# Reordering the first units of a chunked RWKV-7 kernel with a mixture of experts behind it

## The chip, the core and the metric

The kernel runs on one core of a Trainium2 chip. The metric is the device time of one execution in microseconds. Three timed executions of the kernel before gave 1142.85, 1146.27 and 1148.96 us; the median, 1146.27 us, is the time before. The execution that left the profile took 1141.15 us, and its span in the profile is 1139.1 us. The engines are called as in the profile: PE is TensorE (matrix products), DVE is VectorE, ACT is ScalarE, POOL is GpSimd, SP is SyncE, which issues most of the transfers.

## What is computed

The first half of the reference is a recurrence. For each of 4 batches and 8 heads, a 40x40 state goes through 768 tokens:

```python
for t in range(S):
    y[:, :, t] = einsum('bhd,bhde->bhe', r_t, state)
    Sa    = einsum('bhde,bhe->bhd', state, a_t)
    state = state * w_t[:, :, None, :] - einsum('bhd,bhe->bhde', Sa, b_t)
    state = state + einsum('bhd,bhe->bhde', v_t, k_t)
```

The second half takes y, as a matrix x of 3072 tokens by 320 (8 heads of 40), through 4 experts:

```python
p = domain_probs / (domain_probs.sum(-1, keepdims=True) + 1e-09)
for e in range(E):                          # E = 4
    h = np.maximum(x @ w1[e], 0.0)          # 320 -> 1024
    out += p[:, e:e+1] * (h @ w2[e])        # 1024 -> 320
```

All of it is in float32.

## The kernel before, in words

**Units.** The 768 tokens are cut into 12 chunks of 64. A unit is one chunk of two batches (64 + 64 tokens on the 128 partitions, all 8 heads), so there are 24 units; units 0 and 1 are the first chunk of batches 0, 1 and 2, 3. Within a chunk the recurrence becomes products of small matrices and the inverse of a unit triangular 64x64 matrix for each head and batch. Each unit goes through four generators, whose `yield`s are the places where other work can be put between:

- `within` makes what doesn't need the state. It has these steps: the running product of the decays, G (two transposes of rawW, a scan at L401, on DVE); its transpose `pg` on PE and the division `gp`; the scaled keys `n_tok`, `k_tok` and `AT`; their transposes `pNT`, `pKT`; the scores `pc` between R and V (masked on DVE into VC, L382); the scores `pfe` and `pe` (L478 to L485; `pfe` is copied by ACT into F, and `pe` is masked on DVE into ET); the product `pev` of ET and V (copied by ACT into EV).
- `substitute` inverts the 32x32 diagonal blocks of F by forward substitution: ACT and DVE gather `blocks`, DVE transposes them into M (L519) and prepares M and Z (L531, L535). The substitution proper (L540 to L557) runs on DVE for units 0 and 1 and on GpSimd for all others.
- `merge` puts the inverted 32x32 blocks together to 64x64: two transposes on DVE, Qc (L568) and QTc (L570), four copies on GpSimd, then the products `pY` and `pQ` on PE, each followed by copies on ACT.
- `step` takes the state along: `prn` (products with the state, carried in), RH on DVE, `psat` and `pst`, then `pxr` (R with the solution and with the state), masked on DVE into SX, then `pdy`, Y and the new state on DVE, and at last x, transposed by the products `pxT` for the first two chunks and by transfers for the others.

**The experts.** `up` computes relu(x w1) with the products `ph` (L726, L734); `down` of units 0 and 1 computes `po` (L775). From the second chunk on, two units are taken together, with Winograd's form of Strassen's scheme for the second product (`p`, L841), for which `add_weights` (L802) makes sums of w2 on DVE in passing. The weights w1 are streamed from HBM for each unit or chunk in pieces of 640 KB (`load_piece`). All such pieces of work wait in the list `todo`; `mix(n)` takes n of them.

**The order.** Each engine runs its own queue in order. The order is written out by hand in two parts, L939 to L1014 for the first units and the loop L1021 to L1087 for the rest, by how many steps of which generator are run when (`run(gen, n)`). A scheduler may move an instruction between that and the queue, unless `keep_in_program_order` pins it. Among the pinned ones are Qc and QTc, the blocks and M, the masks of VC and ET up to unit 3, and the G, `n_tok`, `k_tok` and AT of the first units.

In pass u of the loop, unit u goes through its step (`s`), unit u+1 through its merge (`m`) and the beginning of its step (`s_next`), unit u+2 through the scores (`w`) and the substitution, and unit u+3 begins. What is left of unit u+1's `within` at the pass's start (`w_next`) is its last product, `pev`. `gap(n)` gives PE pieces of the experts' work; gap 0 is the first. The call `run(sum_ops, ...)` in it makes sums of w2 at the places that `sums_at` names.

**Spare products.** `keep_warm(n)` (L933) puts n products of the identity with itself into PE's queue, each in two passes (two records). Their result isn't used. There are three such calls: 16 at the start, 10 behind the first `pg`, and 18 in front of the first merge's `pY`.

**Buffers.** All accumulators but those of the experts come from one ring of five banks (`big`, L72). `banks` takes two. A new taker waits for the readers of the one that is five takes older. For unit 0, `pe` has banks of its own; for all others it shares those of `pfe`. rawW, rawA, rawV and rawR are one buffer each: the next unit's transfer into them waits for the transpose that reads them.

Of the kernel before, what the change touches and what calls it, by code (L numbers as in the profile page):

```python
# [15 lines left out]
def kernel(  # L16
# [154 lines left out]
    def begin(u):  # L171
        q = Unit()
        q.u, q.c, q.bp = u, u // (B // 2), u % (B // 2)
        q.b = [2 * q.bp, 2 * q.bp + 1]
        q.start, q.end = q.c == 0, q.c == NC - 1
        q.n = {}
        units.append(q)
        return q
# [9 lines left out]
    def load_raw(q, names):  # L188


        moves = []
        for x in names:
            q.n["raw" + x] = t = raw[x]()
            heads = srcs[x].rearrange("b h t e -> (b h) t e")[q.b[0] * H:(q.b[1] + 1) * H, q.c * L:(q.c + 1) * L, :]
            heads = heads.rearrange("n (x two) e -> x n (two e)", two=2)
            for r in range(2):
                if x in "RV":

                    sets = ((slice(0, 8, 2), slice(r, 16, 4)), (slice(1, 8, 2), slice(3 - r, 16, 4)))
                else:  # L200
                    sets = ((slice(0, 8), slice(r, 16, 2)),)
                for n, hs in sets:
                    for y, w_ in enumerate((D + Q, 2 * D - Q)):
                        o = slice(64 * r + Q * y, 64 * r + Q * y + Q)
                        moves.append(lambda eng, out=t[o, n, 0:w_], in_=heads[:, hs, Q * y:Q * y + w_]: eng.dma_start(out=out, in_=in_))
        return moves
# [10 lines left out]
    def go(moves, eng=None):  # L217
        for move in moves:
            move(eng or nc.sync)
# [43 lines left out]
    def load_piece():  # L263

        k = len(pieces)
        e, x = k // 2 % E, k % 2
        if k in in_sums:
            t = sums[in_sums[k]]
        else:
            t = sb.tile([P, PIECE], FP32, name="w1p", tag="w1p", bufs=2)  # L270
        q = Piece()
        q.main = t[:, 0:2 * HF * P].rearrange("p (g c) -> p g c", g=2)
        q.last = t[:, 2 * HF * P:PIECE].rearrange("p (f c) -> p f c", c=P)
        cols = slice(x * HF * P, (x + 1) * HF * P)
        moves = [(q.main, moe_w1[e, 0:2 * P, cols].rearrange("(g p) c -> p g c", p=P))]
        for i in range(2):
            half_cols = slice((2 * x + i) * HF // 2 * P, (2 * x + i + 1) * HF // 2 * P)
            moves.append(
                (q.last[i * DT:(i + 1) * DT], moe_w1[e, 2 * P:DM, half_cols].rearrange("d (f c) -> d f c", c=P))
            )  # L280
        for to, src in moves:
            tc.keep_in_program_order(nc.sync.dma_start(out=to, in_=src))
        pieces.append(q)
# [14 lines left out]
    def load_w2(e):  # L298
        tc.keep_in_program_order(nc.sync.dma_start(out=w2_sb[e][:], in_=moe_w2[e].rearrange("(f p) d -> p f d", p=P)))
# [62 lines left out]
    def banks(name):  # L362
        return [big(f"{name}{x}") for x in range(2)]
# [20 lines left out]
    def within(q):  # L384

        n = q.n
# [91 lines left out]
        pf = quadrants(p, 0, BY_TOKENS, L, lambda j, s, i: (  # L478
            s, i ^ s, j, of_slots(q.AT, s, j, i), of_pairs(NT, s, j, i),
        ))  # L480
        if q.u == 0:
            p = banks("pe")
        pe = quadrants(p, NJ * L, BY_TOKENS, L, lambda j, s, i: (
            s, i, j, of_pairs(KT, s, j, i), of_slots(q.AT, s, j, i),
# [78 lines left out]
    def merge(q):  # L563


        Qc = sb.tile([P, H, Q], FP32, name="Qc", tag="q", bufs=2)
        QTc = sb.tile([P, H, Q], FP32, name="QTc", tag="q", bufs=2)
        tc.keep_in_program_order(nc.vector.transpose(out=dealt(Qc[:]), in_=q.Z))  # L568
        tc.keep_in_program_order(
            nc.vector.transpose(  # L570
                out=QTc[:].rearrange("p h r -> p (h r)"), in_=Qc[:].rearrange("p h c -> p (h c)"),
            )
        )
        q.QT = QTs()
        for i in range(P // Q):
            ins = nc.gpsimd.tensor_copy(out=q.QT[quarter(i), :, quarter(i % 2)], in_=QTc[quarter(i)])  # L576
            tc.keep_in_program_order(ins)
        yield

        py = big("pY")  # L580
        for h in range(H):
            for i in (1, 3):
                nc.tensor.matmul(  # L583
                    out=py[quarter(i - 1), h * Q:(h + 1) * Q], lhsT=q.F[quarter(i), h, 0:Q],
                    rhs=QTc[quarter(i), h, :], start=True, stop=True,
                )
        Y = sb.tile([P, H, Q], FP32, name="Yq")
        for i in (0, 2):
            nc.scalar.copy(out=Y[quarter(i)].rearrange("p h t -> p (h t)"), in_=py[quarter(i), 0:H * Q])
        yield  # L590

        pq = big("pQ")
        for h in range(H):
            for i in (0, 2):
                nc.tensor.matmul(  # L595
                    out=pq[quarter(i), h * Q:(h + 1) * Q], lhsT=Qc[quarter(i), h, :],
                    rhs=Y[quarter(i), h, :], start=True, stop=True,
                )
        for i in (0, 2):
            nc.scalar.copy(out=q.QT[quarter(i), :, quarter(1)], in_=by(pq[quarter(i), 0:H * Q], Q))  # L600
        yield
# [306 lines left out]
    def mix(n):  # L908

        for piece in todo[:n]:  # L910
            piece()
            begin_later(3 if n > 1 else 6)
        del todo[:n]

    def run(gen, n=99):
        if gen is None:
            return
        for _ in range(n):
            if next(gen, gen) is gen:
                break  # L920
# [3 lines left out]
    def begin_step(u):  # L924
        q = units[u]
        if q.bp == 0:
            chunks_x[q.c] = sb.tile([P, 3, 2 * P], FP32, name="xT", tag="xT", bufs=2)
        q.xT = chunks_x[q.c][:, :, q.bp * P:(q.bp + 1) * P]
        return step(q, q.xT)
# [3 lines left out]
    def keep_warm(n):  # L933

        for _ in range(n):
            ins = nc.tensor.matmul(out=warm[:, 0:P], lhsT=ident[:], rhs=ident[:], start=True, stop=True)
            tc.keep_in_program_order(ins)

    ws = [within(units[u]) for u in range(3)]  # L939
# [23 lines left out]
    m, s = merge(units[0]), begin_step(0)  # L963
# [6 lines left out]
    load_piece()  # L970
    run(ws[1], 1)
    run(norm, 1)
    keep_warm(18)
    run(ws[1], 1)
    run(m)
    run(ws[2], 1)
    run(norm)
    load(units[2], "BK")
    go(load_raw(units[2], "A"))
    go(load_raw(begin(3), "W"))  # L980
    load_w2(0)
    load_piece()
    load_piece()
    load_w2(1)
    load_piece()
    run(s, 2)
    run(ws[1], 1)
    run(s)
    run(ws[1], 2)

# [8 lines left out]
    m, s = merge(units[1]), begin_step(1)  # L999
# [15 lines left out]

    sparse = range(4 * 1, 4 * 4 + 2)

    sums_at = {4 * 2 + n: 1 for n in range(1, 11)}
    sums_at.update({4 * 4 + 3: 2, 4 * 5 + 0: 3, 4 * 5 + 1: 2, 4 * 5 + 2: 3})
    sum_ops = (None for e in range(E) for _ in add_weights(e))  # L1020
    for u in range(1, NU):  # L1021
        q = units[u]
        m = s_next = w = w_next = iter(())
        if u + 1 < NU:
            m, s_next = merge(units[u + 1]), begin_step(u + 1)
            w_next = ws[u + 1]
        if u + 2 < NU:
            w = ws[u + 2]

        def gap(n, pieces=None):  # L1030
            at = 4 * u + n
            run(sum_ops, sums_at.get(at, 0))
            mix((1 if at in sparse else 2) if pieces is None else pieces)

        run(w_next)
        run(s, 1)
        gap(0)


        early = u < 5  # L1040
        if early:
            run(s, 1)
        run(w, 1)
        run(s)
        if u == 1:
            mixture_of_unit(q)
        elif q.bp:
            mixture_of_chunk(units[u - 1:u + 1], chunks_x[q.c])
        begin_later(len(later))
        run(w, 1)  # L1050
        if not early:
            run(m, 1)
        gap(1)

        if u + 3 < NU:
            go(load_raw(begin(u + 3), "WA"))
            load(units[u + 3], "WBKV")
            later.extend(load_raw(units[u + 3], "VR"))
        run(w, 2)
        if early:  # L1060
            run(m, 1)
        else:
            run(s_next, 1)
            run(m, 1)
        gap(2)

        if not early:
            run(m, 1)
        run(w, 1)
        if not early:  # L1070
            run(s_next, 1)
        if u + 2 < NU:
            substitute(units[u + 2], nc.gpsimd)
        run(w, 1)
        if u + 3 < NU:
            ws.append(within(units[u + 3]))
            run(ws[u + 3], 1)
        if early:
            run(m, 1)
            run(s_next, 1)  # L1080
            run(m)
            gap(3, 1)
            run(s_next, 1)
            mix(0 if 4 * u + 3 in sparse else 1)
        else:
            gap(3)
        s = s_next  # L1087
# [31 lines left out]
```

## Time and profile before

| engine | busy, us | share of 1139.1 us |
|---|---|---|
| PE | 1099.4 | 97% |
| DVE | 757.8 | 67% |
| POOL | 473.6 | 42% |
| ACT | 338.0 | 30% |

| stretch, us | PE busy, us | mean granted clock |
|---|---|---|
| 0 to 20 | 10.81 | 0.98 |
| 20 to 40 | 15.53 | 0.59 |
| 40 to 60 | 17.62 | 1.00 |
| 60 to 160 | 95.02 | 1.00 |
| 160 to 180 | 16.29 | 1.00 |
| 180 to 200 | 15.14 | 0.75 |
| 200 to 260 | 57.67 | 1.00 |
| 260 to 1100 | 836.3 | 1.00 |
| 1100 to 1139 | 35.00 | 1.00 |

The first table says that PE is the engine with the least room. The second says where the room is: in the first 260 us, in which the pipeline of units fills. The granted clock is the share of its full speed at which PE was allowed to run.

A row of the profile's time line reads: start, duration, engine, line of the kernel, operation, out<-in, shapes, count, and in brackets how long the engine stood idle before it and which instruction of which engine ended that. PE counts two records for one float32 product.

### The profile page before, as it was taken

Reading aid. Unit: us, or ns where it says so; the run is one execution under the profiler, and the core shown is the slowest. Engines: PE = TensorE matmul, PEld = TensorE weight load, DVE = VectorE, ACT = ScalarE, POOL = GpSimd, SP = SyncE. Lnnn points to the kernel's source line nnn. Section 1 sums busy time; section 2 is a strip of 40 time slices with the busy share of each in tenths; the row PEclk is TensorE's granted clock in tenths of the full one; section 3 lists DMA queues with packets and bytes.
Section 4 is the critical chain, followed back from the end, with each engine's and each line's share of the span. In section 5 each row is a group of like instructions: output and inputs, shape, how many; then the busy total and the mean of one; then the engine's idle time right before and its main releaser. Section 6 shows DMA issues by size and latency. Waiting matters only on the chain.

```text
span 1139.1 us, 38245 instructions
## 1 busy us (share of the span) xinstructions
PE 1099.4 (97%) x16036; PEld 976.6 (86%) x16036; DVE 757.8 (67%) x1553; ACT 338.0 (30%) x860; POOL 473.6 (42%) x1221
## 2 busy tenths in 40 slices
PE   6899997999999999999999999999999999999998
PEld 5777776888998989889899898888989898888887
DVE  8756647697767768667677677677677586553343
ACT  2333333333233232332332332332332322311110
POOL 4005626662724635625526526437337246340000
PEclk8899998999999999999999999999999999999999
DMA  7784643254263454444453453443543442231330
GB/s 118 213 245 124 131 99 78 65 132 101 76 146 89 107 128 100 119 122 101 115 121 83 123 118 86 118 102 84 139 102 87 117 110 64 75 90 55 105 92 12
DMA packets 268867, 122.16 MB, mean 107 GB/s; under 512 B 213737, under 2 KB 242073, under 8 KB 268697
## 3 DMA queue, kind: packets, MB, share of 16 engines
q1 hardware_dynamic: 265416, 119.12, 42.7%
q8 instruction: 126, 2.06, 0.8%
q10 hardware_dynamic: 3280, 0.61, 0.3%
q14 instruction: 45, 0.36, 0.1%
HBM read 111.79 MB, written 3.93 MB: 102 GB/s over the span
## 4 chain that ended last, share of the span: by engine, by line
PE 87%; DVE 4%; SPq 2%; DMA 2%; POOL 2%; ACT 2%; issue 1%; DVEq 0%; ACTq 0%
PE ph L734 29%; PE p L841 28%; PE ph L726 9%; PE pdy L371 4%; PE pfe L371 2%; PE psat L371 2%; PE pxr L371 2%; PE prn L371 2%; PE po L775 2%; PE pQ L595 1%; PE pc L371 1%; PE pY L583 1%; PE pev L371 1%; POOL Z L557 1%; PE pg L335 1%
## 5 line engine op out<-in xcount | busy, mean ns | idle before, releaser
L734 PE MATMUL ph<-xT,w1p 128*128 128x256 f32 (+1 forms) x1520 | 344.1, 379 | 2.2 <-issue 2.2
L734 PEld LDWEIGHTS ph<-xT,w1p 128*128 128x128 f32 x1520 | 274.3, 190 | 65.1 <-issue 27.3
L544 POOL TENSOR_TENSOR Z<-M,Z 128x62 f32<-128x62 f32 (+7 forms) x352 | 143.3, 407 | 368.6 <-DVE M L535 336.0
L557 POOL TENSOR_TENSOR Z<-Z 128x31 f32<-128x31 f32 (+7 forms) x704 | 257.2, 365 | 55.2
L835 DVE TENSOR_TENSOR a<-hs 128x512 f32<-128x512 f32 x220 | 152.4, 710 | 128.2 <-ACT hs L739 128.2
L739 ACT ACTIVATE hs<-ph 128x512 f32<-128x512 f32 (+1 forms) x208 | 115.7, 564 | 295.5 <-PE ph L734 295.1
L841 PE MATMUL p<-sums,a 128*128 128x160 f32 x1056 | 165.1, 299 | 0.0
L752 DVE SCALAR_TENSOR_TENSOR osb<-p,gate,osb 128x320 f32<-128x320 f32 (+1 forms) x243 | 107.9, 481 | 74.9 <-PE p L841 70.9
L841 PEld LDWEIGHTS p<-sums,a 128*128 128x128 f32 x1056 | 152.9, 190 | 2.3
L726 PE MATMUL ph<-xT,w1p 64*128 64x256 f32 (+1 forms) x760 | 110.1, 398 | 1.2 <-issue 1.1
L841 PE MATMUL p<-w,hs 128*128 128x160 f32 x704 | 102.9, 299 | 0.0
L841 PE MATMUL p<-w,a 128*128 128x160 f32 x704 | 102.8, 299 | 0.0
L841 PEld LDWEIGHTS p<-w,hs 128*128 128x128 f32 x704 | 100.3, 190 | 2.2
L841 PEld LDWEIGHTS p<-w,a 128*128 128x128 f32 x704 | 98.0, 190 | 0.0
L576 POOL COPY QT<-QTc 32x256 f32<-32x256 f32 x96 | 51.6, 537 | 111.5 <-DVE QTc L570 103.7
L726 PEld LDWEIGHTS ph<-xT,w1p 64*128 64x128 f32 x760 | 67.8, 187 | 14.4 <-issue 4.4
L519 DVE STREAM_TRANSPOSE M<-blocks 128x1024 f32<-128x1024 f32 x24 | 47.0, 1957 | 23.1 <-ACT blocks L516 23.0
L414 DVE RECIPROCAL gp<-gp 128x320 f32<-128x320 f32 x24 | 51.7, 2152 | 0.8
L504 ACT COPY EV<-pev 64x160 f32<-64x160 f32 x96 | 23.4, 286 | 66.8 <-PE pev L371 66.3
L371 PE MATMUL pdy<-VC,k_tok 64*64 64x104 f32 (+1 forms) x768 | 41.6, 260 | 0.1
L600 ACT COPY QT<-pQ 32x256 f32<-32x256 f32 x48 | 17.4, 362 | 79.3 <-PE pQ L595 78.8
L626 ACT COPY SN<-prn 128x256 f32<-128x256 f32 x44 | 15.7, 370 | 84.1 <-DVE RH L621 81.9
(148 smaller groups left out, 1364.0 us busy)
## 6 DMA issues: line engine op xcount, KB each, us to landing
w1p<-in_moe_w_dram SPq DMA_DIRECT2D x95, 512.0 KB
w1p<-in_moe_w_dram SPq DMA_DIRECT2D x190, 64.0 KB
w<-in_moe_w_dram SPq DMA_DIRECT2D x4, 1280.0 KB
sums<-in_moe_w_dram SPq DMA_DIRECT2D x9, 512.0 KB
natW<-in_w_dram SPq DMA_DIRECT2D x48, 80.0 KB
natB<-in_b_dram SPq DMA_DIRECT2D x48, 80.0 KB
natK<-in_k_dram SPq DMA_DIRECT2D x48, 80.0 KB
out_dram<-osb SPq DMA_DIRECT2D x46, 80.0 KB
```

The costliest lines, as they stand in the source:

```text
L371: nc.tensor.matmul(out=p[row][half(col), lo + at * out_cols:lo + (at + 1) * out_cols], lhsT=lhsT, rhs=rhs, start=(n == 0), stop=(n == len( ...
L414: pin(nc.vector.reciprocal(out=gp[:], in_=gp[:]))
L519: ins = nc.vector.transpose(out=M[:], in_=cols)
L544: ins = eng.tensor_tensor(out=Z[:, 1:3, 0:n, j + 1:Q], in0=M[:, j:j + 2, None, j + 1:Q].to_broadcast([P, 2, n, m]), in1=Z[:, here, 0:n, j: ...
L557: eng.tensor_tensor(out=z[:, 0], in0=z[:, 0], in1=z[:, x], op=ALU.add)
L576: ins = nc.gpsimd.tensor_copy(out=q.QT[quarter(i), :, quarter(i % 2)], in_=QTc[quarter(i)])
L726: nc.tensor.matmul(out=ph[i][:, f, :], lhsT=w1.last[i * DT:(i + 1) * DT, f, :], rhs=xT[i * DT:(i + 1) * DT, 2, :], start=(f == 0), stop=False,
L734: nc.tensor.matmul(out=ph[i][:, f, :], lhsT=w1.main[:, g, at * P:(at + 1) * P], rhs=xT[:, g, :], start=False, stop=(g == 1 and f == HF // ...
L739: nc.scalar.activation(out=h[:, i * HF // 2:(i + 1) * HF // 2, 0:n], in_=ph[i][:], func=ACTF.Relu,)
L752: nc.vector.scalar_tensor_tensor(out=to, in0=p, scalar=sc, in1=to, op0=ALU.mult, op1=ALU.add)
L835: nc.vector.tensor_tensor(out=t[:], in0=x, in1=y, op=op)
L841: nc.tensor.matmul(out=p[:, n * HD:(n + 1) * HD], lhsT=a[:, f, :], rhs=b[:, f, :], start=(f == 0), stop=(f == HF - 1),)
```

## The change

It has five parts.

1. In front of the first merge stand 2 spare products in place of 18.
2. Unit 2's first step (its G, on DVE) is moved behind unit 0's whole step, so that DVE has unit 0's masks, Y and state first. The transfer of rawW for unit 3, which needs unit 2's G to be done, is moved behind two pieces of w1. The steps of `s` and of unit 1's `within` between them are split anew.
3. `pe` gets banks of its own for units 0 and 1 (`q.start`), not for unit 0 alone.
4. In each first gap of the loop, the third step of `s` (`pxr`, and the products with the state carried in) goes ahead of `w_next` (`pev`, from the scores).
5. In passes 1 and 2 the first step of the merge (Qc and QTc) goes ahead of the scores `pc` of unit u+2, where it came behind them. And the sums of w2 are dealt to slightly earlier gaps.

Parts 1 to 3 are meant to bring unit 0's x, which the experts wait for, forward; part 4 to have unit u's masks under way while PE does `pev`; part 5 to have the merge's transposes done before it is their turn.

```diff
@@ within
-        if q.u == 0:
+        if q.start:
             p = banks("pe")
@@ the first units
     run(norm, 1)
-    keep_warm(18)
+    keep_warm(2)
     run(ws[1], 1)
     run(m)
-    run(ws[2], 1)
+    run(s, 2)
+    run(ws[1], 1)
+    run(s, 1)
     run(norm)
     load(units[2], "BK")
     go(load_raw(units[2], "A"))
-    go(load_raw(begin(3), "W"))
     load_w2(0)
     load_piece()
     load_piece()
+    run(s, 1)
+    run(ws[2], 1)
+    go(load_raw(begin(3), "W"))
     load_w2(1)
     load_piece()
-    run(s, 2)
-    run(ws[1], 1)
     run(s)
     run(ws[1], 2)
@@ the loop
-    sums_at = {4 * 2 + n: 1 for n in range(1, 11)}
-    sums_at.update({4 * 4 + 3: 2, 4 * 5 + 0: 3, 4 * 5 + 1: 2, 4 * 5 + 2: 3})
+    sums_at = {4 * 2 + n: 2 if n == 4 else 1 for n in range(1, 10)}
+    sums_at.update({4 * 4 + 2: 2, 4 * 4 + 3: 3, 4 * 5 + 0: 2, 4 * 5 + 1: 3})
...
+        run(s, 1)
         run(w_next)
-        run(s, 1)
         gap(0)
...
-        run(w, 2)
+        run(w, 1)
+        if u < 3:
+            run(m, 1)
+        run(w, 1)
         if early:
-            run(m, 1)
+            run(m, 1 if u >= 3 else 0)
         else:
             run(s_next, 1)
             run(m, 1)
```

## The prediction

> **What bounds the kernel now.** I read the page first (shares and slices), then TensorE's waits, then the stretches in order of time around the places that the diff moves.
>
> ```profile
> PE 1099.4 (97%) x16036; PEld 976.6 (86%) x16036; DVE 757.8 (67%) x1553; ACT 338.0 (30%) x860; POOL 473.6 (42%) x1221
> PE   6899997999999999999999999999999999999998
> PEclk8899998999999999999999999999999999999999
> ```
>
> TensorE is busy 97% of 1139.1 us, in each slice after the first eight nine tenths or more until the last. From 260 to 1100 us the table by stage gives it 836 busy of 840 us. So a reordering pays or costs only where TensorE idles or runs at a low clock: before about 260 us. What TensorE gains or loses there, the end gains or loses. The slices at 20 to 40 us and about 190 us have a clock under full; one-microsecond stretches place its changes:
>
> ```profile
> 36.00:37.00 1.00, 1.00 (x9) 0.83 0.00 0
> 190.00:191.00 1.00, 0.00 (x0) 0.50 0.82 122
> 200.00:201.00 1.00, 1.00 (x5) 0.91 0.00 0
> ```
>
> (Columns: stretch, its length, TensorE busy and records, granted clock, DMA share, GB/s.) Solving the means for the switch gives half clock from 19.3 to 36.3 us and from 190.0 to 200.2. The spare products stand in the first of these:
>
> ```profile
> 32.43 6.14 PE L936 MATMUL warm<-ident 128*128 128x128 f32 x36
> 32.56 0.45 DVE L570 STREAM_TRANSPOSE QTc<-Qc 128x256 f32<-128x256 f32 x1
> 37.81 0.69 DVE L458 TENSOR_TENSOR AT<-AT,G 128x512 f32<-128x512 f32 x1
> 38.49 0.69 PE L583 MATMUL pY<-QTc,F 32*32 32x32 f32 x32
> ```
>
> QTc, which pY reads, is done at 33.0, but the 18 spare products (36 records) hold the queue until 38.5. They are also the work during which the clock came up.
>
> The third place is unit 2's merge in the loop's pass u = 1, where VectorE waits for GpSimd's substitution:
>
> ```profile
> 110.02 0.70 DVE L223 STREAM_TRANSPOSE RT<-rawR 128x512 f32<-128x512 f32 x1
> 111.62 0.69 PE L371 MATMUL pc<-RT,VT 40*64 40x64 f32 x32
> 112.40 0.77 DVE L382 COPY_PREDICATED VC<-mask_up,pc 128x256 f32<-128x256 int32 x2 [1.68 <-PE pc L371]
> 115.02 0.51 POOL L557 TENSOR_TENSOR Z<-Z 128x8 f32<-128x8 f32 x2
> 115.57 0.62 DVE L568 STREAM_TRANSPOSE Qc<-Z 128x256 f32<-128x256 f32 x1 [2.40 <-POOL Z L557]
> 116.22 0.45 DVE L570 STREAM_TRANSPOSE QTc<-Qc 128x256 f32<-128x256 f32 x1
> ```
>
> Qc sits 2.40 us at the head of VectorE's queue until GpSimd ends at 115.5 (it began at 94.60: 20.9 us). RT, pc and VC, unit 3's scores, had passed before it.
>
> **What the Trainium skill says.** "TensorE: Matmul & The Clock Gate", Part 1 (What's actually happening): the clock is halved by default, is released after about one busy window and taken back after an idle one; windows last 3413 ns and run free. The trace agrees: the switches above lie 17.06, 153.6 and 10.2 us apart, which is 5, 45 and 3 windows. It adds what the page doesn't: 190 to 200 us has TensorE busy from 191.9 on with 32x32 and 64x64 products, and the clock rose only after a window of full-width ones. The same page (Architectural detail, at the engines' queue depths) says that VectorE is strictly first in, first out; the 2.40 us above is that.
>
> **The change part by part**, from the order of instructions that the changed program has.
>
> *16 spare products fewer.* pY can start at about 33.1: 5.4 us earlier. But its successors now run at half clock. Trace pairs, full and half: pY 0.69 and 1.07 us, a group of four transposes 0.60 and 1.06 (pVT at 84.4 and 22.0), pev 0.67 and 1.32. Step by step: pY 33.1-34.2; copy of Y 0.75, pQ about 1.0, copy of QT, so that psat starts at 36.5; psat and pst 2.5 in place of 1.5, to 39.3 (before 42.8); pNT and pKT 2.1 in place of 1.1, to 41.4 (43.8); pxr 1.3, SX's first masked copy done at 43.15 (44.9); pdy, 2.0 us from there in before, 4.0 at half, ends 47.1. Before it ended at 47.03. If the clock comes up midway (a boundary near 43.2), it ends at 45.1; if it stays down to the ph products, pxT, pc, pfe and pe lose another 1 to 2 us. I take no gain at pdy's end; ends: 2.1 earlier to 1.5 later.
>
> *Unit 2's G behind the first x* (38.42 to 41.15, 2.7 us of VectorE). It lay beside pY and pQ. Now it stands between the state, done at 48.7, and VC, which ran at 50.23: VC starts at 51.45. With pe in banks of its own, pe's second bank takes the buffer of pc, which VC must have read: pe waits from 50.4 to 51.9, and behind it stand the ph products. Hidden partly: before, 0.81 us of idle followed at 51.6. F no longer waits for pe, 0.45 us, but M stands behind VC and blocks in VectorE's queue, 52.85 in place of 52.64. pev, now after one bank of products, waits 0.9 us for ET. Against that, TensorE idled 1.72 us at 65.7 for osb, which now stands two instructions earlier. Sum with the first part: about -0.3 us, ends -2.7 and +1.5.
>
> *pxr before pev.* From unit 4 on TensorE is full and both are needed later: 0. In pass 1 it costs: before, 0.72 + 1.16 us of ph stood between po and pev, and still pev waited:
>
> ```profile
> 94.94 0.28 PE L371 MATMUL pev<-VC,ET 64*64 64x40 f32 x2 [0.82 <-DVE ET L382]
> ```
>
> Now 0.69 (pxr) and 0.5 (three ph) stand there: arrival 93.5, wait 1.4, so +0.6. Passes 2 to 4: pxr comes straight after psat and waits some 0.3 us for SaT's copy, pev then covers SX's mask: 0.
>
> *Merge ahead of the scores, u = 1.* VectorE's new order is VT, AT, osb, Qc, QTc, RT, VC. Queued behind Qc's wait are RT and VC; pc waits for RT; everything of TensorE stands behind pc. GpSimd's end doesn't move against TensorE: its start hangs on M, and M on pfe at 87.8, with the same work before. Qc 115.5-116.1, QTc to 116.6, RT to 117.3, pc at 117.35. TensorE gets to pc at 111.62 + 0.6 = 112.2. It stands 5.1 us. pY follows pc by the same work as before, so nothing is given back: QTc was ready for it anyway. Bounds: 4 (GpSimd faster while VectorE stands) to 5.7.
>
> *The same, u = 2.* GpSimd ends at 143.46, VectorE reaches Qc at 142.9: wait 0.5, nothing behind it urgent (VT, for 159.0).
>
> ```profile
> 161.62 0.69 PE L583 MATMUL pY<-QTc,F 32*32 32x32 f32 x32 [0.96 <-DVE QTc L570]
> 163.57 1.91 DVE L519 STREAM_TRANSPOSE M<-blocks 128x1024 f32<-128x1024 f32 x1
> 166.21 0.30 PE L371 MATMUL psat<-QT,RH 64*64 64x64 f32 x2 [1.44 <-DVE RH L621]
> ```
>
> Qc and QTc (0.60 + 0.45) leave VectorE's path to M, RH and psat, and pY no longer waits 0.96: -1.0 us. The wait at 187 (4.86 us, for GpSimd's unit 4) hangs on M too and moves along: 0.
>
> *Clock after the new gap.* The gap at 187 to 191.9 took the clock down; 5.1 us is as long. It holds a whole window of 3.41 in (5.1 - 3.41) / 3.41 = half of the phases, and a nearly empty one in some more; one or two windows at half clock then cost 1.7 to 3.4 us. Estimate from these: +1.0, ends 0 and 3.5.
>
> *The rest.* sums_at moves w2's sums by one place in passes 2 to 5; VectorE has 33% idle: 0. rawW for unit 3 two pieces later: needed by G at 95, 0.
>
> Sum: -0.3 + 0.6 + 5.1 - 1.0 + 1.0 = +5.4 us; with rounding of the pieces 1146.3 + 5.2 = 1151.5.
>
> **The rivals.**
> *Cold all through* (20%): clock low from 19 us until the ph products, and again after the new gap: 1.5 + 0.6 + 5.1 - 1.0 + 3.5 = +9.7, 1156. For it: small products didn't raise the clock at 191.9 to 196.8. Against: pdy fills all four quadrants.
> *No stall* (16%): GpSimd's substitution ends before TensorE needs pc, because TensorE is held up elsewhere or VectorE's idleness lets GpSimd run faster: -0.3 + 0.6 - 1.0 = -0.7, 1145.6. Against: it would need 5 of 20.9 us.
> *Gain carried* (12%), the other side: the clock is up already (the free windows straddle the idle stretch of 14.8 to 20.7), 5 us won at pY, kept to pdy, no stall: -5 - 1.0 = 1140.3. For it: that idle stretch, 5.9 us, misses a whole window in a quarter of phases. It also needs the stall absent.
> Forecast 52%.
>
> **How the numbers follow.** 1151.5 is the forecast's. Half a per cent is 5.7 us, a line at 1152: of the forecast somewhat under half lies above, with the cold rival's 0.2 makes 0.45; faster 0.11; same 0.44. The four times of before spread over 7.8 us (1141.15 to 1148.96). Range: from just under the no-stall case, 1144, to 1157, over the cold case; what is left out is mainly the gain carried.
>
> **What would show it.** Right: in pass 1 TensorE idle about 5 us in front of pc, put down to RT, and Qc waiting some 4.5 us for GpSimd with RT behind it; pY of the first merge at 33 and 1.07 us long; pdy of unit 0 ending near 47; pY of unit 3 without a wait. Wrong: pc of unit 3 without a wait, or pdy of unit 0 ending before 45 at full clock. The forecast falls if the cost of the queue order in pass 1 is under 2 us.

## The result and the profile after

Three timed executions of the changed kernel gave 1161.53, 1162.02 and 1163.34 us, the one that left the profile 1168.7; the median of the four is 1162.68 us. The ratio to the kernel before is 1.0154, with an interval of 1.0116 to 1.0192: some 17.6 us slower. The forecast, 1151.5 us, had the sign and a third of the size, and the time lies above its range. The trace of the kernel after is of the slowest of its four executions, the trace of before is of the fastest: between the two traces lie more than 17.6 us.

The page of the kernel after, the rows that answer to those shown of before (busy time; busy tenths by slice; granted clock by slice):

```profile
PE 1114.9 (96%) x16004; PEld 987.3 (85%) x16004; DVE 755.9 (65%) x1553; ACT 341.9 (29%) x860; POOL 473.2 (41%) x1221
PE   6798998889999999999999999999999999999998
PEclk8798797999999899999999999999999999999999
```

TensorE's busy time rose by 15.5 us although it has 32 records fewer, and in the profiled executions the span rose by 27.8 us (1139.1 to 1166.9), so idle time rose by 12.3. Busy time that grows with less work points to the clock, and the clock's row shows it: counted from 0, slices 0, 1, 3, 4, 6 and 13 stand at 7 or 8, where before 0, 1 and 6 stood at 8. One-microsecond stretches of the kernel after (stretch, length, five engines' busy time, granted clock, DMA share, GB/s) place some of the changes:

```profile
93.00:94.00 1.00, 1.00 (x31) 0.92 (x32) 0.89 (x5) 0.13 (x1) 0.82 (x3) 0.54 0.82 272
113.00:114.00 1.00, 0.19 (x8) 0.19 (x12) 0.76 (x2) 0.00 (x0) 0.69 (x2) 0.78 0.76 122
123.00:124.00 1.00, 1.00 (x42) 0.87 (x34) 0.10 (x1) 0.75 (x3) 0.00 (x0) 0.60 0.91 280
127.00:128.00 1.00, 0.74 (x21) 0.55 (x22) 1.00 (x4) 0.37 (x1) 0.00 (x0) 0.61 0.39 80
```

Solved for the switches as in the prediction, the means give a clock at half from 18.0 to 41.9 us, 93.1 to 96.5, 113.6 to 123.8, 127.2 to 134.0, 175.0 to 185.2, and in four shorter stretches up to 793 us. Before it was at half in two stretches up to 1100 us.

The first merge in the kernel after, where the 16 spare products are gone:

```profile
32.57 1.22 PE L936 MATMUL warm<-ident 128*128 128x128 f32 x4
32.72 0.45 DVE L570 STREAM_TRANSPOSE QTc<-Qc 128x256 f32<-128x256 f32 x1
33.73 1.06 PE L583 MATMUL pY<-QTc,F 32*32 32x32 f32 x32
```

pY starts at 33.73 (before 38.49) and takes 1.06 us at half clock, both as forecast. And pass 1, unit 2's merge, in the kernel after:

```profile
111.48 0.51 POOL L557 TENSOR_TENSOR Z<-Z 128x8 f32<-128x8 f32 x2
112.03 0.61 DVE L568 STREAM_TRANSPOSE Qc<-Z 128x256 f32<-128x256 f32 x1 [2.69 <-POOL Z L557]
113.05 0.71 DVE L223 STREAM_TRANSPOSE RT<-rawR 128x512 f32<-128x512 f32 x1
113.81 1.13 PE L371 MATMUL pc<-RT,VT 40*64 40x64 f32 x32 [2.83 <-DVE RT L223]
```

Qc waits for GpSimd, RT stands behind Qc, and pc waits for RT. This is the forecast's chain, but the wait is 2.83 us and not 5.1, because TensorE itself came late. What the forecast had nothing of is in the table of TensorE's waits (waiting product, what it waited for, us in total, times, longest). Kernel after:

```profile
PE psat L371 <- issue: 7.0, 4, 3.1
PE prn L371 <- issue: 4.1, 2, 2.1
PE ph L726 <- issue: 3.2, 2, 1.9
```

Kernel before:

```profile
PE psat L371 <- issue: 3.1, 3, 1.5
PE ph L734 <- issue: 2.2, 2, 1.1
PE ph L726 <- issue: 1.1, 2, 0.8
```

"issue" means that the profile shows nothing that the engine waited for. All such waits of TensorE make 6.4 us before and 16.0 after.

### The profile page after: what moved, and what is told of

The parts are those of the page before. It is cut to its first block, busy times and chain, and to the rows that moved or that the text cites. A ratio compares the mean times of both kernels' runs of the same rounds, so it can differ in the third digit from the quotient of the medians.

```text
span 1166.9 us, 38162 instructions
## 1 busy us (share of the span) xinstructions
PE 1114.9 (96%) x16004; PEld 987.3 (85%) x16004; DVE 755.9 (65%) x1553; ACT 341.9 (29%) x860; POOL 473.2 (41%) x1221
## 3 DMA queue, kind: packets, MB, share of 16 engines
q8 instruction: 126, 2.06, 0.8%
## 4 chain that ended last, share of the span: by engine, by line
PE 89%; DVE 6%; issue 2%; ACT 1%; DMA 1%; SPq 0%; DVEq 0%; ACTq 0%
PE ph L734 30%; PE p L841 28%; PE ph L726 9%; PE pdy L371 4%; PE po L775 3%; PE psat L371 2%; PE pfe L371 2%; PE pxr L371 2%; PE prn L371 2%; PE pc L371 1%; PE pQ L595 1%; PE pY L583 1%; PE pev L371 1%; PE pNT L335 1%; PE pKT L335 1%
## 5 line engine op out<-in xcount | busy, mean ns | idle before, releaser
L667 ACT COPY RS<-pxr 64x256 f32<-64x256 f32 x88 | 32.2, 366 | 94.9 <-DMA rawR<-in_r_dram 41.8
L414 DVE RECIPROCAL gp<-gp 128x320 f32<-128x320 f32 x24 | 51.6, 2151 | 0.7
L775 PE MATMUL po<-w,hs 128*128 128x320 f32 x128 | 43.2, 486 | 0.0
L371 PE MATMUL pdy<-SX,n_tok 64*64 64x104 f32 (+1 forms) x768 | 40.2, 252 | 2.1 <-DVE SX L382 2.1
```

What stands on the lines that cost most here:

```text
L371: nc.tensor.matmul(out=p[row][half(col), lo + at * out_cols:lo + (at + 1) * out_cols], lhsT=lhsT, rhs=rhs, start=(n == 0), stop=(n == len( ...
L414: pin(nc.vector.reciprocal(out=gp[:], in_=gp[:]))
L775: nc.tensor.matmul(out=po[:], lhsT=hs[e][f // HF][:, f % HF, 0:P], rhs=w2_sb[e][:, f, :], start=(f == 0), stop=(f == NF - 1),)
```

## The experiments

Ratios are to the kernel before, timed on the same chip beside each kernel; each has its 95% interval. A hundredth is 11.4 us.

### Which part costs what

Three kernels leave out parts of the change, and a fourth has one part alone. Without part 5's merge order:

```diff
-        run(w, 1)
-        if u < 3:
-            run(m, 1)
-        run(w, 1)
+        run(w, 2)
         if early:
-            run(m, 1 if u >= 3 else 0)
+            run(m, 1)
```

> The changed kernel with the merge's transposes behind the scores again in passes 1 and 2; TensorE's and ScalarE's queues are the changed kernel's, only VectorE's order differs. Theory (the queue order on VectorE stops TensorE once, and the clock lost in that gap and after it multiplies the loss): the wait of 2.83 us before unit 3's pc goes, and with it the half clock behind it; 1152 to 1156 us. Rival (the products carried in ahead of the scores' do the damage by themselves): under 3 us gained, 1160 or more. Rival (this order is the whole loss): within 3 us of before, 1146.

Measured: 1154.47 us, 1.0078 (1.0051 to 1.0106).

Without part 4:

```diff
-        run(s, 1)
         run(w_next)
+        run(s, 1)
         gap(0)
```

> The changed kernel with pev ahead of pxr again in each first gap. Theory: the half clock at 93 to 96 us and the waits of pdy for RS go, but TensorE still stops for unit 3's RT, now for about 5 us since it gets there earlier; 1153 to 1158 us. Rival (the order in the first gap is the whole loss): 1146. Rival (it costs nothing, the merge's order is all): 1160 or more.

Measured: 1153.38 us, 1.0083 (1.0055 to 1.0110). pc waited 5.62 us for RT at 114.41, as the forecast had it (5.1).

Without both edits, so parts 1 to 3 and the dealing of the sums alone:

> The changed kernel with both orders as before; left of the change are the fewer spare products, unit 2's G behind the first x, the banks of pe and the sums of w2. Theory: the 3 us that the changed kernel had won at the second merge's pY carry to the end, 1141 to 1145 us. Rival (the lost spare products themselves leave the clock low or put the instruction fetches in bad places): 1150 or more.

Measured: 1148.87 us, 1.0032 (1.0017 to 1.0048). And the kernel before with the first edit of the change alone, `keep_warm(2)` for `keep_warm(18)`:

> The kernel before with 2 spare products in place of 18 in front of the first merge, and nothing else changed. Theory: 1 to 3 us won at unit 0's x, as the clock comes up only during pdy, then carried: 1143 to 1147. Rival (the spare products pay for themselves by the clock): 1149 or more.

Measured: 1151.10 us, 1.0059 (1.0042 to 1.0076). The last two are slower than I expected, by some 4 us each. So parts 4 and 5 each cost some 5 to 6 us over the 1.0032, but leaving out 16 products that compute nothing, and that took 4.9 us of TensorE's time, costs 6.7 us by itself. In the trace of this last kernel, against the one of before, unit 1's merge is 0.6 us late, unit 8's 6.6, unit 23's 9.8: the loss comes in steps long after the place of the edit, at waits named issue (120.61, 165.85, 285.1, 597.4 us and others).

### Borders in TensorE's instructions

I counted TensorE's records in the trace (loads of weights, products, semaphore instructions) up to the end of each wait named issue of over 0.8 us; the last column is what is left when the count is divided by 256:

```
kernel   wait ends   us     count    count mod 256
before     52.41    0.81     1218       194
before    130.13    1.11     3521       193
before    412.50    0.96    12225       193
before    719.44    1.55    21698       194
before    854.43    1.10    25793       193
after     127.26    2.11     3009       193
after     174.69    2.02     4290       194
after     297.71    1.24     8130       194
after     479.28    2.12    13506       194
after     613.76    1.15    17602       194
after     789.26    3.10    22978       194
after     966.44    1.23    28354       194
```

Two of the waits named issue don't fit: the one at 387.02 us of the kernel after, 1.94 us, has 76, and 0.55 us ahead of the first psat, in both kernels, has 136 and 72. For the rest: every 256 instructions TensorE passes a border, and at some of the borders it stands. The largest of these waits, in the kernel after:

```profile
785.50 0.65 PE L371 MATMUL psat<-RH,QT 64*64 64x40 f32 x29
789.26 0.25 PE L371 MATMUL psat<-RH,QT 64*64 64x40 f32 x1 [3.10 <-issue]
```

It splits a run of psat of which all products have the same inputs: the 30th has nothing to wait for that the 29 ahead of it didn't have. The DMA queues of the kernel after from 784.1 to 786.8 us, and from 786.8 to 788.0 (packets, MB, share of 16 engines):

```profile
q1 hardware_dynamic: 551, 0.58, 88.2%
...
q1 hardware_dynamic: 532, 0.21, 70.4%
q8 instruction: 1, 0.02, 5.4%
```

One packet on the queue called instruction comes while TensorE stands and ends (787.9) some 1.3 us before it goes on. The queue has 126 packets of 2.06 MB in all, 16 KB each: 256 instructions of 64 bytes. The Trainium skill, "Runtime: NRT & Kernel Launch", section "Instruction fetch mechanics", says just this of the blocks, 16 KiB or 256 instructions, fetched by the sequencer while it executes the ones before. It calls a crossing "mostly hidden". Here it is hidden where the products are wide: of the 253 borders of these two kernels, the 199 behind a block that lasted over 5.5 us show no wait. Where 256 instructions in a row are small products, they are soon gone (in 2.1 us here, from 784.02 to 786.15), and TensorE may have to wait for the next block. It doesn't always: of the 20 borders behind a block of under 3 us, 9 show a wait. What tells them apart is when the packet comes. The one that ends at 787.9 started 2.9 us after TensorE had passed the border before; the one for the block from 654.9 us on, behind a block that was as quick (2.0 us), had started 0.9 us ahead of that border, and there is no wait. What sets the packet's start the traces don't show.

One spare product is 4 instructions, two loads and two products. Leaving out 16 moves every later border by 64 instructions, a quarter of a block. This can be tested with tiny products, which hardly take time:

```diff
+    def count_on(n):
+        for _ in range(n):
+            ins = nc.tensor.matmul(out=warm[0:Q, 0:8], lhsT=ident[0:Q, 0:Q], rhs=ident[0:Q, 0:8], start=True, stop=True)
+            tc.keep_in_program_order(ins)
...
+        if q.u == 0:
+            count_on(48)
         q.EV = EVs()
```

They stand ahead of the first unit's pev, where TensorE idles anyway. 48 of them in the kernel before (192 instructions) put the borders where 16 spare products fewer put them:

> The kernel before with all its 18 spare products, and 48 tiny products (32x8, 4 TensorE instructions each, so 192 instructions) written ahead of the first unit's pev, where TensorE stands 5.9 us in the trace of before. Why: in the traces of before and after, every wait of TensorE named issue that stands in a run of small products ends when the count of TensorE's instructions is 192 to 194 more than a multiple of 256, some 1.4 us after a packet of the queue called instruction. 192 more instructions put these borders where 16 spare products fewer (64 instructions fewer) put them. Theory 1, the borders (instruction fetch): time about that of the kernel with 2 spare products (1151.1), 1149 to 1154, with waits named issue of 1 to 2 us at the same products as there. Theory 2, the spare products kept the clock up: nothing is taken from them here, so 1144 to 1147.

Measured: 1150.92 us, 1.0064 (1.0045 to 1.0082). 16 in the kernel with 2 spare products:

> 2 spare products in place of 18 and 16 tiny products (64 TensorE instructions) ahead of the first unit's pev in TensorE's idle time, so that the borders of 256 instructions lie after that where they lie in the kernel before. Theory 1 (borders): back to about the time before, 1143 to 1147. Theory 2 (the spare products' warming of the clock): stays at 1149 to 1153, as with 2 spare products alone.

Measured: 1144.24 us, 1.0004 (0.9991 to 1.0018). 16 in the kernel after:

> The kernel after, with 16 tiny products ahead of the first unit's pev: 64 TensorE instructions more, as many as the 16 spare products had that it leaves out. Theory 1 (borders): of the 14 us of waits named issue in its trace some 5 to 8 go, and with them some of the clock's drops: 1152 to 1158. Theory 2: no more than a tenth of that, 1161 to 1164.

Measured: 1154.69 us, 1.0094 (1.0058 to 1.0130). 16 in the kernel without parts 4 and 5:

> The kernel after without its parts 4 and 5 (1148.9 as it was), with 16 tiny products ahead of the first unit's pev. Theory 1 (borders): it keeps the 3 us that the front part gains before the second unit's merge and no longer loses them: 1140 to 1144, faster than both kernels. Theory 2: 1147 to 1150.

Measured: 1140.13 us, 0.9973 (0.9959 to 0.9988), faster than both kernels. The first theory has all four; the spare products' warming is refuted by the first two. The tiny products do nothing else at their place that the trace of the first shows: up to the first merge (38.48 us) and the end of the first half clock (36.3) it goes as before. The pairs differ by 7.3, 6.3, 6.9 and 6.8 us for the same shift; the intervals leave about 3 us either way in each, and 6 in the third, that of the kernel after. The products prn behind unit 3's merge in three of these traces, first the kernel with 2 spare products alone:

```profile
164.33 0.66 PE L371 MATMUL prn<-state,AT 64*64 64x40 f32 x27
165.85 0.26 PE L371 MATMUL prn<-state,AT 64*64 64x40 f32 x3 [0.86 <-issue]
```

Kernel before with 48 tiny products:

```profile
161.52 0.66 PE L371 MATMUL prn<-state,AT 64*64 64x40 f32 x27
164.57 0.33 PE L371 MATMUL prn<-state,AT 64*64 64x40 f32 x3 [2.40 <-issue]
```

2 spare products and 16 tiny ones:

```profile
165.71 0.68 PE L371 MATMUL prn<-state,AT 64*64 64x40 f32 x32
166.19 0.67 PE L371 MATMUL prn<-ident,state 64*64 64x64 f32 x32
```

The first two stand behind the same 27th record of prn, in different kernels; in the third the border lies elsewhere. The waits named issue sum to 11.0, 12.0 and 6.9 us in these three, to 8.5 and 5.2 in the kernel without parts 4 and 5 and its tiny-product version, to 16.0 and 3.9 in the kernel after and its. In each pair, the kernel with the borders moved has more of these waits, by 3.3 to 12.1 us. A trace is of one execution and the 6 to 7 us are of medians, so the difference can't be split into waits and clock: after the first 45 us, the clock is at half 17 us longer in two of the pairs, 3.4 us longer in one, and equally long in the one of the kernels with 2 spare products.

### Parts 4 and 5 with the borders kept

From here each kernel has the 16 tiny products, and each is compared with the last one above, the kernel without parts 4 and 5 at 1140.13 us, called the 1140.1 kernel. Part 4 alone on top of it:

> The kernel after without part 5 (the merge stays behind the scores), with part 4 (carried-in products ahead of pev) and with 16 tiny products ahead of the first unit's pev, so that its borders of 256 instructions lie where those of the kernel before lie. Against 1140.1 without part 4. Theory 1: part 4 costs by itself, since pdy takes the PSUM banks that were taken last but two times, which are now those of pxr and not of pev, and RS is copied from them late: a wait of pdy for RS of 2 to 3 us in the fourth pass, and the clock's drops at that and at the longer wait of pev in the first pass: 1144 to 1148. Rival: part 4 was dear only through the borders (1154.5 against 1148.9 there): 1140 to 1142.

Measured: 1148.22 us, 1.0032 (1.0019 to 1.0046): 0.0059 over 0.9973, 6.7 us. Part 5 alone:

> The kernel after without part 4, with part 5 (the merge's transposes ahead of the scores' in passes 1 and 2) and with 16 tiny products, against 1140.1 without part 5. Theory 1: pc of unit 3 waits some 5.5 us for RT in the first pass as it did without the tiny products (5.62), the clock drops behind it, and 1 to 2 us come back in pass 2, where pY no longer waits: 1144 to 1147. Rival (part 5 was dear through the borders): 1140 to 1142.

Measured: 1149.13 us, 1.0039 (1.0025 to 1.0053): 7.6 us, more than the expected 4 to 7. Its trace has the forecast's stall at full length, and what follows it:

```profile
112.10 0.61 DVE L570 STREAM_TRANSPOSE Qc<-Z 128x256 f32<-128x256 f32 x1 [5.57 <-POOL Z L559]
113.89 1.13 PE L371 MATMUL pc<-RT,VT 40*64 40x64 f32 x32 [5.62 <-DVE RT L223]
```

and, in the table of stretches (the last three columns are the granted clock, the DMA share and GB/s):

```profile
113.00:122.00 9.00, 8.11 (x84) 7.10 (x88) 1.61 (x4) 0.77 (x2) 1.98 (x5) 0.50 0.71 137
```

The clock is at half from 112.6 to 122.8 us, three windows. From pc's start that is 8.9 us at half speed, by which I estimate 4.45 us lost. 5.62 + 4.45 = 10.1; the next merge is 9.8 us later than in the 1140.1 kernel, and some 3 come back by the merge after. If the stall is the cost, part 5 in pass 2 alone must be free of it:

```diff
-        if u < 3:
+        if u == 2:
             run(m, 1)
...
-            run(m, 1 if u >= 3 else 0)
+            run(m, 0 if u == 2 else 1)
```

> The 1140.1 kernel with part 5 in the second pass alone, where GpSimd is done early: on VectorE Qc and QTc of unit 3 run ahead of VT, RT and VC's copies of unit 4, nothing else moves. Theory 1: pY of unit 3 no longer waits 0.96 us for QTc, and psat behind it less: 1138 to 1140. Rival (RT comes later and holds pc, as in the first pass): 1141 to 1144.

Measured: 1139.66 us, 0.9958 (0.9944 to 0.9972), the lowest ratio of all, though its interval and the 1140.1 kernel's overlap. pY of unit 3 doesn't wait, and psat behind it waits 0.68 us in place of 1.44.

### Where part 4 costs

In the trace of part 4 alone, pev of pass 1 waits 1.20 us in place of 0.82, near the forecast (1.4), and then comes the clock. Its row and a stretch behind it:

```profile
91.27 0.30 PE L371 MATMUL pev<-VC,ET 64*64 64x40 f32 x2 [1.20 <-DVE ET L382]
```

```profile
93.00:95.00 2.00, 2.00 (x29) 1.92 (x25) 1.58 (x4) 0.95 (x4) 1.77 (x3) 0.50 0.74 256
```

The same of the 1140.1 kernel:

```profile
91.37 0.28 PE L371 MATMUL pev<-VC,ET 64*64 64x40 f32 x2 [0.82 <-DVE ET L382]
```

```profile
91.00:96.00 5.00, 4.63 (x92) 4.18 (x93) 3.66 (x10) 1.55 (x6) 4.20 (x11) 1.00 0.62 159
```

One window at half, 1.7 us, and 0.4 of wait make 2.1; the next merge is 2.3 us later. A second place is pdy near 249 us, which waits 2.64 us for RS where it waited 0.93 for SX. I suspected pdy's PSUM banks. The first try took pxr's banks from the pool ahead of pev's:

```diff
+        q.px = banks("pxr")
         run(w_next)
         run(s, 1)
```

> The 1140.1 kernel (parts 4 and 5 left out, 16 tiny products) with one thing changed: the two PSUM banks of pxr are taken from the ring of five ahead of the two of pev. All instructions and their order on every engine stay; pdy, which comes next but one in the ring, then gets the banks of pxr instead of those of pev. Theory 1 (the banks are what part 4 costs in the fourth pass): pdy's first product waits for RS, 1.5 to 3 us of idle in the fourth pass where 0.9 stood, with a drop of the clock: 1142 to 1146. Rival (the order of pxr and pev itself, or nothing): 1140 to 1141, with pdy waiting 0.9 us for SX as before.

Measured: 1141.65 us, 0.9976 (0.9962 to 0.9989). The edit changed nothing: the trace has the same instructions with the same semaphores on every engine, and pdy waits for SX here too (1.53 us). So asking for banks earlier doesn't change which banks are given. It is a second timing of the 1140.1 kernel. The next try wrote a tiny product into both of pxr's banks ahead of pev, in pass 4:

> The 1140.1 kernel with one tiny product into each of pxr's two banks ahead of pev in the fourth pass (2 fewer at the front), so that pxr takes its banks ahead of pev and pdy, next but one in the ring of five, gets pxr's banks; the order of the other products is nearly the same. Theory (banks): pdy's first product in the fourth pass waits 2 to 3 us for RS in place of 0.9 us for SX, perhaps with a drop of the clock: 1142 to 1144. Rival (the order itself): wait of about 0.9 us, 1140 to 1141.

Measured: 1142.51 us, 0.9982 (0.9969 to 0.9994), and no wait for RS. It was in the wrong pass and decides nothing: the wait near 249 us is unit 5's, in pass 5. Part 4 in passes 5 and later alone:

```diff
-        run(s, 1)
+        if u >= 5:
+            run(s, 1)
         run(w_next)
+        if not (u >= 5):
+            run(s, 1)
```

and, with the conditions exchanged, in passes 1 to 4 alone:

> The 1140.1 kernel with part 4 in passes 5 to 23 alone. Of the 10 us that the trace with part 4 in all passes lost against it, 6.3 were lost up to the sixth merge and 4.2 at a wait named issue near 900 us with the clock's drop behind it. If the late passes cost by themselves: 1143 to 1146. If they cost nothing, as forecast, and the wait at 900 us is one run's bad luck: 1140 to 1141.

> The 1140.1 kernel with part 4 in passes 1 to 4 alone. If the early passes carry the cost (pev's wait of 1.2 us with a drop of the clock in the first pass, pdy's wait for RS in the fourth): 1145 to 1148. If they carry half of it: 1142 to 1144.

Measured: 1143.43 us, 0.9991 (0.9979 to 1.0003), and 1143.25 us, 0.9988 (0.9976 to 1.0000): 2.1 and 1.7 us. The wait for RS is in the first of these and not in the second. In the first, ScalarE copies RS behind SX's mask and in front of EV. My reading was that pev's banks are read late by this, and pdy is given pxr's. The last run swaps these eight copies in pass 5 alone, nothing else; both groups are pinned, and RS's stand behind a `yield` of their own:

```diff
         if u >= 5:
             run(s, 1)
         run(w_next)
+        if u == 5:
+            run(s, 1)
```

> The kernel with part 4 in passes 5 and later alone (1143.4; pdy of unit 5 waited 2.69 us for RS, and the clock dropped from 247.2 to 250.6), with the four copies of EV ahead of the four of RS on ScalarE in the fifth pass. No other engine's order changes; pdy of unit 5 gets the two PSUM banks of pev in place of those of pxr. Theory (ScalarE's queue and with it the banks): pdy waits 0.9 to 1.6 us for SX, as without part 4, and the sixth merge is 1 to 3 us earlier: 1140 to 1142. Rival (the order of the products itself): the wait stays near 2.7 us, 1143 to 1144.

Measured: 1142.16 us, 0.9970 (0.9955 to 0.9986). The kernel with part 4 from pass 5 on:

```profile
245.10 1.51 ACT L669 COPY RS<-pxr 64x256 f32<-64x256 f32 x4 [5.77 <-DVE SX L382]
245.89 0.39 PE L371 MATMUL pdy<-VC,k_tok 64*64 64x104 f32 x2 [2.69 <-ACT RS L669]
```

The same with EV ahead of RS in pass 5:

```profile
241.45 1.20 ACT L510 COPY EV<-pev 64x160 f32<-64x160 f32 x4 [3.35 <-PE pev L371]
242.09 0.39 PE L371 MATMUL pdy<-VC,k_tok 64*64 64x104 f32 x2
243.82 1.50 ACT L675 COPY RS<-pxr 64x256 f32<-64x256 f32 x4 [1.17 <-DVE SX L382]
243.84 0.30 PE L371 MATMUL pdy<-SX,n_tok 64*64 64x104 f32 x1 [1.36 <-DVE SX L382]
```

EV is copied while SX's mask is still to come, and pdy starts 2.6 us earlier, counted from the merge ahead of it (228.47 and 227.24 us). It starts before RS is copied, so its banks are not pxr's here, though the order in which banks are taken is the same in both kernels. Which banks a new taker gets thus seems to depend on which have been read, and not, as the section on buffers says, on a strict count of five takes.

Of the 2.6 us pdy waits 1.36 again, for SX, and the clock drops for a window in both. From this merge to the next the pass takes 39.65 us in place of 40.94. Where part 4 leaves pass 5 alone, it takes 38.15 us in the 1140.1 kernel and 39.68, also with a drop of the clock, in the one with part 4 in passes 1 to 4. The ratio is 2.4 us lower and back at that without part 4, but the intervals of the two, 0.9955 to 0.9986 and 0.9979 to 1.0003, overlap. So from pass 6 on no cost of part 4 is to be seen. In pass 5 the wait for RS comes from a copy's place in ScalarE's queue, and its removal is worth 1.3 us in the traces; that this is the whole cost there isn't shown.

What stays open: the two halves, 2.1 and 1.7 us, make 3.8 of the 6.7 that part 4 costs in all passes. The four intervals leave 3 us either way, so I can't tell whether 2.9 us come from the two together (the trace with part 4 in all passes has more drops of the clock between 129 and 212 us) or from chance. Holding the clock up through pc's stall with products was not tried.

## Why the prediction was wrong

The time was 17.6 us over before and the forecast 5.2 (the terms of its sum make 5.4). By parts:

| term | forecast, us | measured, us | ratios |
|---|---|---|---|
| parts 1 to 3, borders kept | -0.3 | -3.1 | 0.9973 |
| part 4, borders kept | +0.6 | +6.7 | 1.0032 to 0.9973 |
| part 5, borders kept | 5.1 - 1.0 + 1.0 | +7.6 | 1.0039 to 0.9973 |
| 4 and 5 together | +5.7 | +13.9 | 1.0094 to 0.9973 |
| borders moved by 64 instructions | none | +6.9 | 1.0154 to 1.0094 |

The two steps that failed most are the first two below: instructions were priced by their time alone, which left the moved borders out (+6.9 us), and "pxr before pev" was put at +0.6 us and cost 6.7.

- *"16 spare products fewer", "I take no gain at pdy's end".* Wrong, twice. The clock came up midway (41.9 us), the case that I named beside (pdy's end at 45.1) and didn't choose: pdy ended at 44.90, one of my own signs of being wrong. It was no luck of one execution: in all sixteen traces with 2 spare products the clock comes up between 40.5 and 43.5 us, and pdy ends between 44.2 and 45.2. By itself this gain goes no further: in the two kernels that have the fewer spare products alone, the wait for osb grows from 1.72 to 2.85 us, the second merge is 0.6 us late, and with the borders kept the ratio is 1.0004. With parts 2 and 3 this wait is gone, and the second merge starts 3.05 us earlier. The waits of pe for VC (1.07 us) and of pev for ET (0.88) are near the forecast (1.5 and 0.9). And the step took the products for time alone. As 64 instructions they moved the borders in all that follows, which cost more than the 4.9 us that they took.
- *"pxr before pev": +0.6 in pass 1, 0 elsewhere.* Failed. pev's wait was right (1.20 us for 1.4); the clock that fell with it, an estimated 1.7 us, wasn't in the sum. "From unit 4 on TensorE is full and both are needed later: 0" fails in pass 5, where ScalarE's queue turned the order of two products into 2.7 us of wait. It holds from pass 6 on. Where 2.9 of the 6.7 us come from is open, as said above.
- *"Merge ahead of the scores, u = 1": 5.1.* Right in mechanism and size: 5.62 us where it is alone. In the changed kernel it is 2.83, since pass 1 had already cost TensorE time at pev: it got to pc at 110.98 us, and in the kernel with part 5 alone at 108.27.
- *"The same, u = 2": -1.0.* The mechanism was right: pY is without a wait, and psat's wait is halved. The size isn't shown: 0.9958 against 0.9973, which the intervals don't separate.
- *"Clock after the new gap": +1.0.* The term is mis-sized: an estimated 4.45 us, over my upper end of 3.5. I asked for a window of 3.41 us that is idle, or nearly so, and counted one or two windows at half clock. Less idleness is enough: in the kernel after, TensorE was busy for 25% of the window up to 113.6 us and for 64% of the one up to 93.1, and the clock dropped behind both. And the small products behind the stall kept it down for three windows.
- *The rest: 0.* Right for rawW and the sums, as far as the 0.9973 shows. What was missing altogether is the border. The profile before had it: 6.4 us of waits named issue. The prediction passed over them, and it took one of them, the 0.81 us at 51.6, for slack that hides other work.

Of the rivals, the cold one came nearest in time: more clock was lost than forecast. But it came near by other places than it named: the clock did come up during pdy.

## What to carry to other kernels

Before moving or removing instructions on a full TensorE queue, look where its waits named issue fall: if they come a multiple of 256 instructions apart, a shift of the whole stream by a few dozen instructions can cost or save more than the edit, and tiny products in an idle place set it back. Price a new wait by what the clock does after it too, most of all where small products follow. And when two products change places, follow their copies through the copying engine's queue to the next taker of the banks.

## What the runs showed of the hardware

- A border of 16 KB in TensorE's instructions cost up to 3.1 us where a block's 256 instructions were small products (64x64 and 32x32). The border waits in the table end 1.3 to 1.6 us after the packet's end. Behind blocks of over 5.5 us no border cost anything that can be seen.
- The clock fits how much of the array works better than whether TensorE is busy. The Trainium skill, "TensorE: Matmul & The Clock Gate", Part 1 (What's actually happening), has it taken back after an idle window. In the eighteen traces I summed for each window of 3.41 us up to 300 us the products' columns times their share of the 128x128 array, as a share of 1400 columns per us, a scale on which the widest windows reach 0.86. The clock dropped after 80 windows, all at 0.30 or less and 69 under 0.25, among them the one up to 93.1 us in the kernel after, in which TensorE idled 1.2 us. It stayed at full after 1236, of which 2 were under 0.25. It stayed at half after 144, none over 0.31, 26 of them with TensorE busy throughout with small products. It rose after 80, none under 0.28. The share of busy time doesn't part them so well: TensorE was busy up to 76% in windows after which the clock dropped, and as little as 46% in one that kept it. So the page's rule holds here with "busy" read as some 0.25 to 0.3 on this scale. No run varied this alone.
